# Attention with a threshold mask and an expert layer: the mask's bias on VectorE, the weights loaded as float32 and cast on the chip

## Chip, cores and metric

One Trainium2 chip, one of its cores. The time is the device time of one execution in microseconds (us), as the median of a kernel's timed executions.

## The reference, cut to what matters

```python
def _attn_ref(q, k, v, tau):                      # 8 x 8 heads, 576 rows, head size 64
    scores = scale * np.matmul(q, k.transpose(0, 1, 3, 2))
    thresh = np.max(scores, axis=-1, keepdims=True) - tau
    scores = np.where(scores >= thresh, scores, -1000000000.0)
    ...                                           # softmax
    return np.matmul(attn, v)

def _moe_ref(x, w_in, w_out):                     # x: 4608 x 512, w_in: 512 x 2048, w_out: 2048 x 512
    h = x @ w_in
    relu6 = np.clip(h + 3.0, 0.0, 6.0)
    g = h * relu6 / 6.0
    return g @ w_out
```

## The kernel before

The program is one loop of 144 slots, nine for each group of four heads. A slot takes 128 queries of two heads through the softmax, and puts matrix work of the expert layer between. The scores are compared with their row's maximum through a *bias*, `tau - scale*max`, that a Prelu on ScalarE (the mask) adds: what falls below zero is multiplied by 1e30.

```python
    def load_v(b):                                # float32 in memory, bfloat16 on the chip
        ...
            vcasts.append(lambda g=g: nc.gpsimd.dma_start(out=vm[:, g * 4:g * 4 + 4, :], in_=v[b, ...]))
        ...                                       # two of vm, two of vr for each batch
    def load_weights():                           # 32 pieces of 128 x 512
        for n4 in range(4):
            for ki in range(KI):
                casts.append(lambda n4=n4, ki=ki: nc.gpsimd.dma_start(out=w_in_sb[...], in_=moe_w_in[...]))
        ...                                       # and 16 of w_out

    def sm_max(sl):
        ...
        for i, ps in enumerate(sl.tiles):         # two heads
            nc.vector.tensor_scalar(out=sl.s[...], in0=ps[...], ..., op1=Alu.max, accum_out=sl.m[:, i:i + 1])
            nc.gpsimd.tensor_scalar(out=sl.bias[:, i:i + 1], in0=sl.m[:, i:i + 1], scalar1=-scale, scalar2=tau,
                                    op0=Alu.mult, op1=Alu.add)

    def sm_norm(sl):
        for i in range(2):
            nc.gpsimd.tensor_scalar(out=pn[:, i, :], in0=sl.s[:, i, :], scalar1=sl.rinv[:, i:i + 1], ...)
        ...
        if not sl.on_chip:                        # every second slot before 21: TensorE transposes instead
            nc.sync.dma_start_transpose(out=sl.dst, in_=pn[...])

    load_quad(0)                                  # the loads of q and k, by the sync queue
    start(loads, 5)
    load_v(0)                                     # only lists the loads of v; the loop starts them
    load_weights()
    ...
    queue[0].tiles = scores(0, 0)
    for n, sl in enumerate(queue):
        now = n
        ...
        if slot == 0 and g == 1 and b + 1 < B:
            load_v(b + 1)                         # from the third batch on, its four loads go out in slots 0 to 3
        ...                                       # exp(prev), sm_max(sl), h, ReLU, gate, o
        for i in range(2):
            sm_mask(sl, i)
        ...                                       # transpositions, attention x V, the next scores
        if prev is not None:
            sm_norm(prev)
        flush()
        start(loads, 1)
        if n < 4 or n > 12:
            start(vcasts, 1)
        if n > 3:
            start(casts, 1 if n < 24 else 2)
        prev = sl
```

## Time and profile before

| | before |
|---|---|
| time, median (lowest to highest) | 560.16 us (559.52 to 560.89) |
| span and mean granted TensorE clock of the profiled run | 558.7 us, 0.996 |
| busy: TensorE, VectorE, ScalarE, GpSimd | 530.6, 424.7, 469.7, 305.3 us |
| first mask | 9.71 us |
| slots 4-14, 14-18, 18-23 | 29.51, 13.79, 15.19 us |
| slots 23-31, 31-36 | 29.74, 17.27 us |
| slots 36-143, then the tail | 373.87, 57.3 us |

Slots are dated from ScalarE's timeline, by the first mask activation of each: "slots 14-18" runs from the mask of slot 14 to that of slot 18. Where one slot's time is given ("slot 16 took"), it runs from the mask of the slot before to its own. The start, the stages (0-4 took 12.30 us) and the tail add up to the span. So a change can be booked by stage, and each stage has its own limit.

### The profile page before, as it was taken

How to read it: one execution, taken by the hardware profiler on the slowest of the kernel's cores; microseconds unless marked ns; L12 is line 12 of the kernel's file. 1: busy time of each engine (PE TensorE's matmuls, PEld its weight loads, DVE VectorE, ACT ScalarE, POOL GpSimd, SP SyncE). 2: the span in 40 equal slices, each digit the busy share in tenths (PEclk: the TensorE clock that was granted, in tenths of full speed). 3: DMA queues.
4: the chain of work that ended last, by engine and by line, in shares of the span. 5: the costliest groups of instructions: out<-in, count | busy, mean ns of one | idle time of the engine just before them, and what ended most of it. 6: DMA issues, size and time to landing. Idle time of an engine off the chain costs nothing.

```text
span 558.7 us, 11624 instructions
## 1 busy us (share of the span) xinstructions
PE 530.6 (95%) x3829; PEld 309.2 (55%) x3870; DVE 424.7 (76%) x1041; ACT 469.7 (84%) x999; POOL 305.3 (55%) x646
## 2 busy tenths in 40 slices
PE   8899798799999999999999999999999999999997
PEld 6655455555555555655555555655555565654663
DVE  3787686787878788887978788887978798883440
ACT  4899899798889999899898999899898999984440
POOL 2788878854556555755556555755556555561000
PEclk9999899999999999999999999999999999999999
DMA  5999979976789869978689889977689865454102
GB/s 121 137 120 173 196 128 190 204 142 126 137 158 152 152 136 157 178 149 146 130 148 152 173 131 160 175 147 147 131 145 166 150 144 114 100 109 94 38 20 76
DMA packets 286348, 77.52 MB, mean 139 GB/s; under 512 B 269264, under 2 KB 281808, under 8 KB 286288
## 3 DMA queue, kind: packets, MB, share of 16 engines
q1 hardware_dynamic: 267680, 67.47, 65.3%
q0 software_dynamic: 17408, 8.92, 13.6%
q8 instruction: 30, 0.49, 0.4%
q10 hardware_dynamic: 1200, 0.39, 0.3%
q14 instruction: 30, 0.25, 0.1%
HBM read 36.70 MB, written 9.44 MB: 83 GB/s over the span
## 4 chain that ended last, share of the span: by engine, by line
PE 55%; DVE 11%; ACT 8%; issue 4%; SPq 3%; DMA 2%; POOL 2%; DVEq 0%; POOLq 0%
PE h L357 17%; PE o L386 16%; PE s L260 15%; DVE s L281 5%; PE av L327 3%; ACT s L289 3%; ACT s L294 3%; DMA nq<-in_q_dram 2%; DVE g L374 2%; DVE r L368 2%; ACT r L366 1%; PE s L266 1%; PE tp L214 1%; SPq L310 1%; POOL pn L302 1%
## 5 line engine op out<-in xcount | busy, mean ns | idle before, releaser
L302 POOL TENSOR_SCALAR pn<-s,rinv 128x576 bf16<-128x576 f32 x288 | 211.6, 745 | 133.1 <-DVE rinv L297 57.3
L289 ACT ACTIVATE s<-s,bias 128x576 f32<-128x576 f32 x288 | 206.9, 766 | 36.3 <-POOL bias L284 35.2
L281 DVE TENSOR_SCALAR_CACHE_REDUCE s<-s 128x576 f32<-128x576 f32 x288 | 205.9, 752 | 40.3 <-PE s L260 29.9
L294 ACT ACTIVATE s<-s 128x576 f32<-128x576 f32 x288 | 192.7, 671 | 0.3
L260 PE MATMUL s<-kT,qT 64*128 64x288 f32 x1024 | 169.7, 430 | 5.1 <-DVE s L281 2.8
L357 PE MATMUL h<-xT,w_in_sb 128*128 128x320 bf16 (+1 forms) x1024 | 144.9, 287 | 5.9 <-DVE g L374 5.0
L386 PE MATMUL o<-w_out_sb,g 128*128 128x512 bf16 x535 | 133.5, 379 | 5.2 <-DVE osb L394 3.0
L357 PEld LDWEIGHTS <-w_in_sb 128*128 128x128 bf16 x1024 | 92.1, 97 | 68.9 <-issue 31.9
L374 DVE SCALAR_TENSOR_TENSOR g<-r,h 128x512 bf16<-128x512 f32 (+1 forms) x128 | 96.4, 755 | 41.7 <-ACT r L366 39.9
L260 PEld LDWEIGHTS s<-kT,qT 64*128 64x128 f32 x1024 | 93.7, 186 | 60.9 <-DVE s L281 24.0
L284 POOL TENSOR_SCALAR bias<-m 128x1 f32<-128x1 f32 x288 | 54.4, 189 | 66.6 <-DVE s L281 45.8
L386 PEld LDWEIGHTS <-g 128*128 128x128 bf16 x576 | 55.6, 98 | 57.4 <-issue 9.0
L366 ACT ACTIVATE r<-h,three 128x640 f32<-128x640 f32 (+1 forms) x74 | 54.4, 736 | 20.6 <-PE h L357 19.9
L294 ACT ACTIVATION_READ_ACCUMULATOR s<-s 128x1 f32 x288 | 54.2, 188 | 0.0
L368 DVE TENSOR_SCALAR r<-h 128x512 f32<-128x512 f32 (+1 forms) x54 | 40.5, 751 | 0.0
L394 DVE TENSOR_SCALAR osb<-o 128x512 f32<-128x512 f32 x31 | 21.0, 676 | 21.4 <-PE o L386 21.4
L327 PE MATMUL av<-pT,vm 128*64 128x512 bf16 x256 | 34.6, 393 | 2.0 <-ACT kT L204 2.0
L327 PEld LDWEIGHTS <-vm 128*64 128x64 bf16 x512 | 18.0, 111 | 25.3 <-issue 18.8
L297 DVE RECIPROCAL rinv<-rsum 128x2 f32<-128x2 f32 x144 | 23.0, 160 | 11.3 <-ACT s L294 10.5
L339 DVE CAST xT<-av 128x512 bf16<-128x512 f32 x32 | 21.8, 681 | 6.6 <-PE av L330 6.3
L281 DVE DVE_READ_ACCUMULATOR s<-s 128x1 f32 x288 | 23.9, 83 | 0.0
L266 PE MATMUL s<-kT,qT 64*64 64x288 f32 x256 | 20.1, 415 | 0.7 <-DVE s L281 0.7
(44 smaller groups left out, 241.4 us busy)
## 6 DMA issues: line engine op xcount, KB each, us to landing
km<-in_k_dram SPq DMA_DIRECT2D x64, 128.0 KB, 3.0
out_dram<-osb SPq DMA_DIRECT2D x31, 256.0 KB, 2.4
nq<-in_q_dram SPq DMA_DIRECT2D x96, 72.0 KB, 2.7
vm<-in_v_dram POOLq DMA_DIRECT2D x16, 256.0 KB, 5.6
w_in_sb<-in_moe_w_in_dram POOLq DMA_DIRECT2D x16, 128.0 KB, 4.3
w_out_sb<-in_moe_w_out_dram POOLq DMA_DIRECT2D x16, 128.0 KB, 4.5
pT<-pn SPq DMA_TRANSPOSE x119, 3.4
nq<-in_q_dram SPq DMA_DIRECT2D x14, 128.0 KB, 4.4
```

Source lines behind the costliest of these rows:

```text
L260: nc.tensor.matmul(tiles[a][:, hf, 0:HALF], qT_of(pair)[a * 64:(a + 1) * 64, t * P:(t + 1) * P], keys(pair, a, hf), start=True, stop=True)
L281: nc.vector.tensor_scalar(out=sl.s[:, i, :].rearrange("p (a b) -> p a b", a=2), in0=ps[:, :, 0:HALF], scalar1=1.0, scalar2=None, op0=Alu.m ...
L284: nc.gpsimd.tensor_scalar(out=sl.bias[:, i:i + 1], in0=sl.m[:, i:i + 1], scalar1=-scale, scalar2=tau, op0=Alu.mult, op1=Alu.add)
L289: nc.scalar.activation(out=s, in_=s, func=Act.Prelu, bias=sl.bias[:, i:i + 1], scale=scale, alpha=REJECT)
L294: nc.scalar.activation(out=s, in_=s, func=Act.Exp, accum_out=sl.rsum[:, i:i + 1])
L302: nc.gpsimd.tensor_scalar(out=pn[:, i, :], in0=sl.s[:, i, :], scalar1=sl.rinv[:, i:i + 1], scalar2=1.0, op0=Alu.mult, op1=Alu.mult)
L327: nc.tensor.matmul(ps[a * 64:(a + 1) * 64, :], vm[:, 2 * hp + a, c * D:(c + 1) * D], pT[:, 5 * a + c, cols], start=(c == 0), stop=False)
L357: nc.tensor.matmul(hps[:, n, 0:w], w_in_sb[:, ki, (ni + n) * P:(ni + n + 1) * P], xT[b][:, ki, c0:c0 + w], start=(ki == 0), stop=(ki == KI ...
L366: nc.scalar.activation(out=r, in_=hps, func=Act.Relu, bias=three[:])
L368: nc.vector.tensor_scalar(out=r, in0=hps, scalar1=3.0, scalar2=0.0, op0=Alu.add, op1=Alu.max)
L374: nc.vector.scalar_tensor_tensor(out=gbuf[:, ni:ni + 2, c0:c0 + w], in0=r, scalar=6.0, in1=hps, op0=Alu.min, op1=Alu.mult)
L386: nc.tensor.matmul(o_ps[0], gbuf[:, ni, mt * P:(mt + 1) * P], w_out_sb[:, ni, :], start=(ni == 0), stop=(ni == NI - 1))
```

## The change

Its intent: GpSimd's queue makes masks wait in the stages in which weights load. So the bias goes to the engine that makes the maximum, and the weights no longer need GpSimd to build a casting DMA. They come as float32 through the sync queue into six staging buffers, and GpSimd casts each piece two slots later.

```diff
+    w_pool = ctx.enter_context(tc.tile_pool(name="wp", bufs=6))
...
-                casts.append(lambda n4=n4, ki=ki: nc.gpsimd.dma_start(
-                    out=w_in_sb[:, ki, n4 * 512:(n4 + 1) * 512],
-                    in_=moe_w_in[ki * P:(ki + 1) * P, n4 * 512:(n4 + 1) * 512]))
+                casts.append(lambda n4=n4, ki=ki: stage(
+                    w_in_sb[:, ki, n4 * 512:(n4 + 1) * 512],
+                    moe_w_in[ki * P:(ki + 1) * P, n4 * 512:(n4 + 1) * 512]))
... (w_out in the same way)
+    def stage(dst, src):
+        w = w_pool.tile([P, 512], F32, tag="w", name="w")
+        nc.sync.dma_start(out=w[:], in_=src)
+        staged.append((now, dst, w))
+
+    def cast_staged():
+        while staged and staged[0][0] <= now - 2:
+            _, dst, w = staged.pop(0)
+            nc.gpsimd.tensor_copy(out=dst, in_=w[:])
...
-            nc.gpsimd.tensor_scalar(out=sl.bias[:, i:i + 1], in0=sl.m[:, i:i + 1], scalar1=-scale, scalar2=tau,
+            nc.vector.tensor_scalar(out=sl.bias[:, i:i + 1], in0=sl.m[:, i:i + 1], scalar1=-scale, scalar2=tau,
...
             sm_norm(prev)
+        cast_staged()
         flush()
```

More of the change, by code (lines that the diff above doesn't have):

```diff
@@ L76 @@
     vcasts = []
+    staged = []
     def load_quad(quad):
@@ L142, in load_weights @@
             for ki in range(KI):
-                casts.append(lambda n4=n4, ki=ki: nc.gpsimd.dma_start(
-                    out=w_in_sb[:, ki, n4 * 512:(n4 + 1) * 512],
-                    in_=moe_w_in[ki * P:(ki + 1) * P, n4 * 512:(n4 + 1) * 512]))
+                casts.append(lambda n4=n4, ki=ki: stage(
+                    w_in_sb[:, ki, n4 * 512:(n4 + 1) * 512],
+                    moe_w_in[ki * P:(ki + 1) * P, n4 * 512:(n4 + 1) * 512]))
         for ni in range(NI):
-            casts.append(lambda ni=ni: nc.gpsimd.dma_start(
-                out=w_out_sb[:, ni, :], in_=moe_w_out[ni * P:(ni + 1) * P, :]))
+            casts.append(lambda ni=ni: stage(w_out_sb[:, ni, :], moe_w_out[ni * P:(ni + 1) * P, :]))
+    def stage(dst, src):
[6 more added lines that the diff above has]
+            nc.gpsimd.tensor_copy(out=dst, in_=w[:])
     def start(jobs, n):
@@ L152, in start @@
             jobs.pop(0)()
+    now = -1
     load_quad(0)
@@ L187, in kT_of @@
         return qkT[pair // 2][1][:, pair % 2, :]
-    now = -1
     turn = 0
```

## The prediction

> **What bounds the kernel now.** I read the page first (busy shares, the 40 slices, the groups), then the busy time by stretch, then the chain of waits and the timelines where a stretch looked unlike its neighbours. A slot is one step of the program: 128 queries of two heads, 144 slots in all; I date slots by the first mask activation (L289) of each in ScalarE's timeline.
>
> ```profile
> PE 530.6 (95%) x3829; PEld 309.2 (55%) x3870; DVE 424.7 (76%) x1041; ACT 469.7 (84%) x999; POOL 305.3 (55%) x646
> ...
> PE   8899798799999999999999999999999999999997
> ...
> POOL 2788878854556555755556555755556555561000
> ```
>
> The shares mix stages. POOL (GpSimd) is 55% busy overall, but 70 to 80% in slices 2 to 8 (14 to 112 us), which is where TensorE shows its only 7s before the end. Those are the slots in which the weights are loaded. The table by stretch (us; PE, PEld, DVE, ACT, POOL busy) shows the two regimes:
>
> ```profile
> 50.00:60.00 10.00, 7.23 (x52) 3.75 (x51) 8.22 (x25) 8.32 (x19) 9.22 (x19) 0.97 1.26 167
> ...
> 100.00:110.00 10.00, 7.59 (x68) 4.59 (x70) 6.40 (x17) 8.41 (x19) 8.68 (x17) 1.00 1.39 208
> ...
> 300.00:350.00 50.00, 49.11 (x376) 28.46 (x379) 42.00 (x107) 46.71 (x102) 27.97 (x61) 1.00 0.89 148
> ```
>
> At 50 to 60 us TensorE is 72% busy and POOL 92%; from 125 us on TensorE is 98% busy and POOL 56%. In the steady stage the chain of waits is TensorE after TensorE:
>
> ```profile
> 255.46 1.19 PE h L357 x8
> 256.66 1.73 PE o L386 x8
> 258.38 1.17 PE s L260 x8
> 259.55 1.19 PE h L357 x8
> ```
>
> In the loading stage it goes through POOL. Its queue is in order, so the bias (L284) of a slot stands behind the normalisation (pn) of an earlier slot and the descriptors of the DMAs issued there, and ScalarE's mask waits for it:
>
> ```profile
> 96.98 0.74 POOL vm L122
> ...
> 97.72 0.81 POOL w_out_sb L147 x2
> ...
> 98.86 0.19 POOL bias L284
> 99.06 0.02 issue
> 99.08 1.44 ACT s L289 x2
> ```
>
> VectorE had finished the maximum of that slot at 96.59 (timeline), so the bias came 2.3 us late, and ScalarE's timeline has it idle 1.40 us before 99.08. The list of waits gives ScalarE's idle time for the bias, one line for each of the stretches 8 to 42, 42 to 78, 78 to 125 and 125 to 500 us (total, times, longest):
>
> ```profile
> ACT s L289 <- POOL bias L284: 4.9, 7, 2.4
> ACT s L289 <- POOL bias L284: 4.0, 7, 1.1
> ACT s L289 <- POOL bias L284: 5.1, 7, 1.4
> ACT s L289 <- POOL bias L284: 20.7, 47, 1.5
> ```
>
> So 14.0 us fall in the early stages, where they cost time, and 20.7 in the one that TensorE bounds, where they mostly do not.
>
> **What the Trainium skill says.** (1) "DMA: Bandwidth & Descriptors", SWDGE vs HWDGE vs iDMA: a DMA that casts must be issued by GpSimd, where software builds the descriptors; plain ones from the sync queue are built in hardware. The trace agrees: each weight DMA (L143, L147) holds POOL for 536 to 596 ns. (2) "VectorE: DVE Perf Modes", The DRAIN you can't avoid: a same-engine read after write needs a semaphore. The changed program has it: every bias waits for VectorE's own semaphore. The trace agrees that dependence costs time (below). (3) "SBUF — State Buffer", Who interferes with whom: VectorE and GpSimd share a port pair, and a tensor_scalar in a two-port mode blocks, or is blocked by, a whole GpSimd instruction. Whether a one-element operation takes that mode, no run here shows. (4) The DMA page again, Issuing engines are not separate DMA queues: the same 16 engines serve all queues, so the weights' traffic is not lightened; the trace has the DMA share at 1.26 and 1.39 in the two early stretches above.
>
> **The change part by part.**
>
> *Removed from POOL:* 288 bias operations of 189 ns, 54 us, and 32 descriptor builds of about 0.57 us, 18 us. *Added to POOL:* 32 casts of 128x512. The normalisation of 128x576 takes 745 ns; in proportion I put a cast at 0.65 us (an estimate), 21 us together. POOL falls from 305 to about 254 us. More important, ScalarE no longer waits for that queue.
>
> *Added to VectorE:* 288 bias operations, between the two maxima of a slot and after the second. Here dependence costs more than the operation:
>
> ```profile
> 260.36 0.08 DVE L281 DVE_READ_ACCUMULATOR s<-s 128x1 f32 x1
> 260.36 0.75 DVE L281 TENSOR_SCALAR_CACHE_REDUCE s<-s 128x576 f32<-128x576 f32 x1
> 261.04 0.08 DVE L281 DVE_READ_ACCUMULATOR s<-s 128x1 f32 x1
> 261.04 0.82 DVE L368 TENSOR_SCALAR r<-h 128x640 f32<-128x640 f32 x1
> 261.89 0.82 DVE L374 SCALAR_TENSOR_TENSOR g<-r,h 128x640 bf16<-128x640 f32 x1
> ```
>
> An operation that depends on nothing before it starts 0.68 us after a maximum of 0.75 started: they overlap. The gate (L374), which reads what L368 wrote, starts 0.03 after its end. A bias must wait for the accumulator read, 0.76 after the maximum's start, plus 0.03; it lasts about 0.16 (the smallest arithmetic in the trace, the reciprocal of 128x2 on L297, has a median of 158 ns), and the next operation can overlap its last 0.08. So the next starts at 0.87 instead of 0.68: 0.19 us for each bias, 0.37 to 0.38 for a slot, 54 us of VectorE's time in all. As busy time less, since part is waiting: I expect VectorE at about 460 us.
>
> *Moved to the sync queue:* 32 loads of 256 KB, at about 0.62 us of issuing each (its other loads take 1.25 for two), 20 us in the slots 4 to 29. They stand in order behind the DMA transposes (1.3 us), which wait for pn.
>
> *Stage 1, slots 4 to 23 (22.0 to 80.5 us).* ScalarE's floor is a mask pair and an exp pair, 1.35 + 1.34 = 2.70 us. Slots 14 to 18 (48.15 to 65.31) take 3.43 each, because POOL does bias, pn, vm or vr and w, 3.3 us, without a gap; without that loop I give them 2.85: 5 x 0.58 = 2.9 us. The other 14 take 2.90 to 3.04; VectorE, 2.4 us of busy time a slot there (46.4 us in the 19.5 slots from 20 to 80 us), rises to 2.75, so it is as tight as ScalarE, and I credit 0.1 each: 1.5 us.
> *Stage 2, slots 23 to 31 (80.5 to 110.2).* 3.72 us each. ScalarE's work is 2.70, 0.62 for a ReLU in half of them, and some copies: 3.2. I credit 0.35 of the 0.5: 2.8 us.
> *From these, the casts take back something:* a load issued at the end of slot n follows pn(n-1), a transpose (1.3), other loads (1.3 to 2.6) and itself (0.6), and lands some 4 us later (3.0 to 4.4 are the medians of such loads): 7 to 8.5 us after pn(n-1). Its cast follows pn(n+1), two slots or 5.7 us later. So POOL can stand for 1 to 2 us at a cast, and pn behind it is late; in the slots up to 22 TensorE transposes every second pn itself and has little spare. I take off 1.5 us. Early stages together: 2.9 + 1.5 + 2.8 - 1.5 = 5.7 us gained.
>
> *Stage 3, slots 36 to 143 (127 to 505 us).* 3.49 us a slot, TensorE bound. VectorE is busy 42.0 of 50, 2.93 a slot; with 0.37 it has 0.19 left. What it can hurt is the gate: the next slot's h matmuls wait for it, since h has one buffer. I took from the two timelines, for each gate, the time from its end to the start of the next h. Where ScalarE does the ReLU, the gate had been waiting for it (25.6 us in 48 waits, 0.53 each), which absorbs 0.37. Where VectorE does (48 gates), 22 have under 0.4 us to spare and the shortfalls against 0.37 sum to 5.0 us. Against that, earlier masks pull some late ReLUs forward: I give 1.5 back. Loss 3.5 us. The tail after 505 us holds no bias and no load and stays.
>
> **Sum:** 560.2 - 5.7 + 3.5 = 558 us.
>
> **The rivals.** *A: POOL's queue was all that mattered,* and VectorE's additions hide. For it: VectorE is 76% busy and waits 25 us for scores in the steady stage. Against: the 22 gates with no spare time. It would give 560 - 7 to 8, about 552. *B: VectorE becomes the second bound of the steady stage:* backlog of one slot meets the next in slots with an output copy (0.6) and a transposition. For it: 0.19 us left of 3.49. Against: a backlog needs consecutive heavy slots, and slot 8 of each nine has no gate. At 0.06 us more a slot it costs another 6 us: 564 to 566. *C: the weights arrive late* and casts hold POOL for long: the sync queue is nearly full in slots 22 to 29 (transpose, loads and two weights, about 4.3 us a slot). For it: DMA share 1.39. Against: pn's four buffers, and the first w_out is only needed at slot 31. The early gain would vanish: 563. *D: the one-element operation takes the shared port* and stands behind pn's 0.75 us: up to 10 or 20 us more, above 571. Nothing in the trace speaks for it.
>
> **Range and chances.** The two terms have opposite signs and similar size, so I stay near the old time: 558 us, 550 to 566 for A to C. Faster by over 2% (below 549.0) needs more than all the early waiting, 8%; slower by over 2% (above 571.4) needs B and C together, or D: 6%; within 2%, 86%.
>
> **What would show it.** Right: no wait of ScalarE for POOL; bias on VectorE near 160 ns, each taking 0.19 us from the row of operations; VectorE near 460 us, POOL near 254; slots 14 to 18 under 3 us and 23 to 31 near 3.4; more and longer waits of h for the gate after 125 us, slots there 3.52 to 3.53. Wrong: a bias far from 160 ns, or stretched beside pn (D); steady slots unchanged (A) or above 3.55 (B); POOL idle for long before casts and early slots no shorter (C).

## More of the kernel before

GpSimd's timeline, TensorE's and ScalarE's of the kernel before (start, duration, engine, line, operation, and in brackets how long the engine had been idle and what ended that):

```profile
5.06 0.63 PE L214 MATMUL tp<-identf,km 128*128 128x128 f32 x4 [0.45 <-DMA km<-in_k_dram]
...
9.48 0.19 POOL L284 TENSOR_SCALAR bias<-m 128x1 f32<-128x1 f32 x1 [8.17 <-DVE s L281]
...
9.71 0.78 ACT L289 ACTIVATE s<-s,bias 128x576 f32<-128x576 f32 x1 [2.44 <-POOL bias L284]
```

TensorE transposes the first keys at 5.06, and GpSimd has nothing to do before the first bias at 9.48. Behind that bias, in the same queue, stands the first load of v; GpSimd began it at 10.40.

## The result, and the profile after

The changed kernel takes 572.19 us (four runs, 571.43 to 573.15) against 560.16. The ratio is 1.0215, 95% interval 1.0201 to 1.0230: slower by just over 2%, and above the predicted range. All results are correct.

Line numbers of the new kernel are 11 higher from the scores on (mask L300, bias L295, pn L313, gate L385, h L368). Its page:

```profile
PE 539.9 (95%) x3870; PEld 313.6 (55%) x3870; DVE 462.8 (81%) x1329; ACT 475.6 (83%) x999; POOL 251.8 (44%) x358
...
PE   7899789989999999999999999999999999999997
PEclk8999699999999999999999999999999999999999
...
POOL 1556665585335434544345444544445445442000
```

The busy times came out as predicted: VectorE 462.8 (predicted 460), GpSimd 251.8 (254), and GpSimd's digits 2 to 8 fell from 7 and 8 to 5 and 6. The sign that something else went wrong is in the clock row, where the slices are 14.3 us wide: an 8 in the first and a 6 in the fifth (57 to 71 us). The booking by stage gives:

| | before | after | difference | predicted |
|---|---|---|---|---|
| first mask | 9.71 | 13.56 | +3.85 | 0 |
| slots 0-4 | 12.30 | 12.48 | +0.18 | 0 |
| 4-14 | 29.51 | 29.43 | -0.08 | parts of -1.5 and -2.9 |
| 14-18 | 13.79 | 17.86 | +4.07 | most of -2.9, part of +1.5 |
| 18-23 | 15.19 | 15.88 | +0.69 | parts of -1.5 and +1.5 |
| 23-31 | 29.74 | 25.61 | -4.13 | -2.8 |
| 31-36 | 17.27 | 20.88 | +3.61 | 0 |
| 36-143 | 373.87 | 377.60 | +3.73 | +3.5 |
| tail | 57.3 | 57.3 | -0.02 | 0 |
| sum | | | +11.9 | -2.2 |

The five slots to which the prediction gives -2.9 run from the mask of slot 13 (48.15) to that of slot 18 (65.31), one slot more than "14-18". Over these five the difference is +3.67.

Each stage is read from one profiled run, so it matters how far a stage moves by chance. Two kernels of the experiments, e7 and e10, issue the same instructions as the kernel before up to slot 36. Against it, their first mask came 0.50 and 0.98 us later, 14-18 took 0.73 and 1.23 less, 31-36 took 0.00 and 1.05 more, and the other early stages moved by under 0.1. One source of this is TensorE's clock. The kernel before has a spell at half clock in stage 14-18, from 59.35 to 62.76 by its clock records; its windows (columns as further below, the clock is the third number from the end):

```profile
58.00:60.00 2.00, 0.98 (x10) 0.32 (x4) 1.96 (x7) 1.85 (x3) 1.82 (x5) 0.84 1.35 209
60.00:62.00 2.00, 1.99 (x13) 1.05 (x15) 0.85 (x4) 1.52 (x5) 1.74 (x5) 0.50 1.37 228
62.00:64.00 2.00, 2.00 (x14) 0.81 (x10) 0.69 (x1) 2.00 (x6) 1.73 (x3) 0.81 1.40 216
```

Slot 18 took 3.91 us there; it took 2.68 in e5, e7 and e10, which have the same bias and no such spell at that point. So 1.2 us of the time that the prediction put down to GpSimd's loop in these slots were a spell of half clock.

The table shows one gain and four losses that are clear of this; three of the losses were not in the working or were far larger than in it. The four losses, one after the other:

**The start.** The same three engines in the new kernel:

```profile
1.45 0.93 POOL L124 DMA_DIRECT2D vm<-in_v_dram  x1
...
7.48 0.63 PE L225 MATMUL tp<-identf,km 128*128 128x128 f32 x4 [2.86 <-DMA km<-in_k_dram]
...
13.56 0.78 ACT L300 ACTIVATE s<-s,bias 128x576 f32<-128x576 f32 x1 [3.32 <-DVE bias L295]
```

The first load of v is no longer held behind a bias, and leaves at 1.45 instead of 10.40. The first keys then reach TensorE 2.42 us later. The other 1.43 us come after that: TensorE's next transpositions (of q) took 1.06 us instead of 0.60, and the recorded clock is 0.59 and 0.56 in the windows 8 to 10 and 10 to 12 us, where it was 1.00 before.

**Slots 14-18.** TensorE, GpSimd and ScalarE at slot 16:

```profile
57.98 0.61 POOL L159 CAST w_in_sb<-w 128x512 bf16<-128x512 f32 x1 [2.58 <-DVE bias L295]
59.38 1.47 POOL L313 TENSOR_SCALAR pn<-s,rinv 128x576 bf16<-128x576 f32 x2
...
60.19 1.43 PE L329 MATMUL pt<-identb,pn 128*128 128x128 bf16 x9 [2.85 <-POOL pn L313]
62.40 2.29 PE L271 MATMUL s<-kT,qT 64*128 64x288 f32 x8
...
65.87 1.58 ACT L300 ACTIVATE s<-s,bias 128x576 f32<-128x576 f32 x2 [4.83 <-DVE bias L295]
```

GpSimd stood idle for 2.58 us at a cast, with the next pn behind it in the queue. (The profile puts that wait down to a bias of VectorE's, which the cast does not read. The cast needs the transfer of w: the one issued at 53.27 landed at 57.93, by the trace, and the cast began at 57.98.) TensorE stood idle 2.85 us for that pn. The windows (us; PE, PEld, DVE, ACT, POOL busy, then clock, DMA share, GB/s) show what followed:

```profile
60.00:65.00 5.00, 4.70 (x23) 2.99 (x23) 1.63 (x3) 1.04 (x4) 3.63 (x6) 0.50 1.24 242
65.00:70.00 5.00, 4.67 (x31) 2.22 (x31) 3.45 (x14) 3.00 (x7) 3.85 (x6) 0.52 1.29 202
```

For 10 us TensorE ran at half its clock, though it was 94% busy. Eight score matmuls took 2.29 us; at full clock and with no wait among them they take 1.24. Slot 16 took 7.59 us.

The Trainium skill, "TensorE: Matmul & The Clock Gate", Part 1: The HAM clock gate, says that TensorE's clock is halved after an idle window of about 3.4 us, and comes back after about as long of steady work. In the length of a spell the traces agree: leaving out the last 10 us of each run, every spell at half clock in the fourteen clock records lasted 3.41 or 3.42 us, or two or three times that (59.56 to 69.80 here, 10.24 us). In what starts a spell they do not. TensorE had been idle for 2.2 us (from 57.33) when the clock fell here, and in the 3.4 us ahead of the spell in the kernel before it was idle for 0.90 us at the longest (58.39 to 59.29). Nor does the idle time decide it alone: after 2.62 us in e3 (114.41 to 117.03) and 2.03 in the kernel before (102.92 to 104.96) the clock stayed at 1.00. That the wait at slot 16 brought this spell is likely, since e3's profile repeats it (2.71 us of idle time, then 10.24 at half clock), but it is not shown.

**Slots 31-36** give back most of what 23-31 gained; the wait there is shown with experiment e1.

**Slots 36-143.** TensorE's waits for the gate in this stage, before and after (engine, line, releaser: total us, times, longest):

```profile
PEld L357 <- DVE g L374: 5.2, 8, 0.8
...
PE h L357 <- DVE g L374: 2.4, 7, 0.4
```

```profile
PEld L368 <- DVE g L385: 12.1, 19, 1.0
...
PE h L368 <- DVE g L385: 3.4, 8, 0.5
PEld s L271 <- DVE bias L295: 10.4, 25, 0.4
```

TensorE's weight loads waited 12.1 us for the gate instead of 5.2, its matmuls 3.4 instead of 2.4. The two overlap, so their sum is not time lost. The last line is new: the weight loads of the scores now wait for the bias too. To see which slots the waits for the gate belong to, I added up both kinds by slot (windows around each h, 7.8 and 15.3 us in all): before, they lie ahead of the h of slots 3 (3.9 us), 7 (2.9) and 4 and 6 (1.0). After, they lie ahead of slots 3 (7.4), 7 (5.9) and 5 (2.0). These follow the gates of slots 2, 6 and 4, whose ReLU VectorE does itself. How much of the +3.73 comes by the gate and how much by the scores is not shown.

### The profile page after: what moved, and what is told of

It is laid out like the page before. It is cut to its first block, busy times and chain, and to the rows that moved or that the text cites. A ratio compares the mean times of both kernels' runs of the same rounds, so it can differ in the third digit from the quotient of the medians.

```text
span 570.6 us, 11793 instructions
## 1 busy us (share of the span) xinstructions
PE 539.9 (95%) x3870; PEld 313.6 (55%) x3870; DVE 462.8 (81%) x1329; ACT 475.6 (83%) x999; POOL 251.8 (44%) x358
## 4 chain that ended last, share of the span: by engine, by line
PE 57%; DVE 21%; ACT 8%; issue 5%; POOL 4%; DMA 4%; SPq 2%; DVEq 0%; POOLq 0%; ACTq 0%
PE s L271 16%; PE o L397 14%; PE h L368 14%; DVE s L292 10%; PE av L338 4%; ACT s L300 3%; DVE g L385 3%; ACT s L305 3%; POOL pn L313 2%; DVE r L379 2%; PE s L277 2%; DMA nq<-in_q_dram 2%; DVE bias L295 2%; PE tp L225 1%; PE warm L177 1%
## 5 line engine op out<-in xcount | busy, mean ns | idle before, releaser
L313 POOL TENSOR_SCALAR pn<-s,rinv 128x576 bf16<-128x576 f32 x288 | 210.9, 744 | 248.6 <-DVE rinv L308 114.6
L292 DVE TENSOR_SCALAR_CACHE_REDUCE s<-s 128x576 f32<-128x576 f32 x288 | 215.4, 748 | 38.1 <-PE s L271 32.3
L300 ACT ACTIVATE s<-s,bias 128x576 f32<-128x576 f32 x288 | 214.4, 769 | 26.8 <-DVE bias L295 21.8
L271 PE MATMUL s<-kT,qT 64*128 64x288 f32 x1024 | 173.8, 433 | 4.9 <-DVE s L292 2.4
L368 PE MATMUL h<-xT,w_in_sb 128*128 128x320 bf16 (+1 forms) x1024 | 145.1, 287 | 6.7 <-DVE g L385 4.9
L397 PE MATMUL o<-w_out_sb,g 128*128 128x512 bf16 x576 | 141.2, 379 | 4.7 <-DVE osb L405 4.4
L271 PEld LDWEIGHTS s<-kT,qT 64*128 64x128 f32 x1024 | 96.6, 187 | 61.3 <-DVE s L292 19.1
L368 PEld LDWEIGHTS <-w_in_sb 128*128 128x128 bf16 x1024 | 91.3, 98 | 70.2 <-issue 29.6
L385 DVE SCALAR_TENSOR_TENSOR g<-r,h 128x512 bf16<-128x512 f32 (+1 forms) x128 | 96.2, 752 | 14.4 <-ACT r L377 10.1
L295 DVE TENSOR_SCALAR bias<-m 128x1 f32<-128x1 f32 x288 | 44.3, 154 | 10.0
L225 PE MATMUL tp<-identf,km 128*128 128x128 f32 x128 | 19.8, 278 | 2.9 <-DMA km<-in_k_dram 2.9
```

The lines of the kernel that those rows point to most:

```text
L271: nc.tensor.matmul(tiles[a][:, hf, 0:HALF], qT_of(pair)[a * 64:(a + 1) * 64, t * P:(t + 1) * P], keys(pair, a, hf), start=True, stop=True)
L292: nc.vector.tensor_scalar(out=sl.s[:, i, :].rearrange("p (a b) -> p a b", a=2), in0=ps[:, :, 0:HALF], scalar1=1.0, scalar2=None, op0=Alu.m ...
L295: nc.vector.tensor_scalar(out=sl.bias[:, i:i + 1], in0=sl.m[:, i:i + 1], scalar1=-scale, scalar2=tau, op0=Alu.mult, op1=Alu.add)
L300: nc.scalar.activation(out=s, in_=s, func=Act.Prelu, bias=sl.bias[:, i:i + 1], scale=scale, alpha=REJECT)
L368: nc.tensor.matmul(hps[:, n, 0:w], w_in_sb[:, ki, (ni + n) * P:(ni + n + 1) * P], xT[b][:, ki, c0:c0 + w], start=(ki == 0), stop=(ki == KI ...
L385: nc.vector.scalar_tensor_tensor(out=gbuf[:, ni:ni + 2, c0:c0 + w], in0=r, scalar=6.0, in1=hps, op0=Alu.min, op1=Alu.mult)
```

## The experiments

Three theories stood at the beginning. *Casts:* late transfers hold GpSimd at the casts (rival C of the prediction), all the rest is small. *Start:* the freed load of v delays the first keys. *VectorE:* the bias costs there far more than its 0.19 us (rivals B and D). Twelve kernels ran, four at a time, each group on one chip with its own runs of the kernel before. Two more, which cast four slots later from twelve buffers, could not be built: they need 24 KB in each partition, and 12.8 KB were left.

### e1 and e2: one half of the change each

e1, from the kernel before:
```diff
-            nc.gpsimd.tensor_scalar(out=sl.bias[:, i:i + 1], ...
+            nc.vector.tensor_scalar(out=sl.bias[:, i:i + 1], ...
```

> The bias moved to VectorE alone; the weights stay cast DMAs issued by GpSimd. Theory 1, from the two traces: the 12 us of the change are four separate things: +3.9 at the start (GpSimd no longer waits for the first bias, so the first load of v is issued at 1.5 instead of 10.4 us and delays the first q and k; first mask at 13.6 instead of 9.7), +4 and +4 from casts that wait for their load and hold pn back (slots 15 to 18 and 31 to 36), +3.7 in the slots 36 to 143 from the bias on VectorE, and -4 in slots 23 to 31. Then this kernel has the start's and the steady stage's loss and the gains, without the casts: 561 to 565 us. Theory 2, VectorE is the bound everywhere and the bias alone is the whole loss: 570 to 573. Theory 3, the weights are the whole loss (their bytes as float32, their place in the sync queue): 556 to 560.

Measured: 570.96 us (567.21 to 574.49), ratio 1.0190 [1.0139, 1.0241]. Start +4.64, slots 14-18 **-1.43**, 18-23 +2.22, 23-31 -4.05, 31-36 +5.10, 36-143 +3.77.

e2, from the changed kernel:
```diff
-            nc.vector.tensor_scalar(out=sl.bias[:, i:i + 1], ...
+            nc.gpsimd.tensor_scalar(out=sl.bias[:, i:i + 1], ...
```

> The weights by the sync queue and cast by GpSimd, the bias left on GpSimd. Theory 1: start as before (first mask at 9.7), slots 36 to 143 as before (3.49 us each), but waits of casts now also hold the bias: 564 to 570 us. Theory 2 (the bias on VectorE is the whole loss): 558 to 562. Theory 3 (the weights are): 570 to 573.

Measured: 571.92 us (569.99 to 572.53), ratio 1.0202 [1.0179, 1.0226]. Start +0.09, 4-14 +3.14, 14-18 +1.13, 23-31 **+7.23**, 31-36 +0.74, 36-143 -0.38.

What follows: each half alone costs about as much as both together, in different places. Both times missed the range of my first theory (561 to 565, 564 to 570) and lie inside that of the theory that makes this half the whole loss. The stages speak against it, as neither half has the losses of the other. The start, the steady stage and the give-back at 31-36 belong to the bias. The stall at 14-18 needs the casts. With the casts but without the bias moved, the biases stand behind waiting casts and the stages of the weights get worse; the moved bias is what turns +7.23 into -4.13 in 23-31. (In e2's stage 23-31 ScalarE waited 11.4 us for the bias, up to 5.2 at a time.) In e1 the bias alone gives -4.05 there, with the weights' DMAs still built by GpSimd. The losses do not add up, so halves of a change cannot be booked by subtracting.

e1 also shows the give-back most clearly. The remainder of slot 26's pn, pR, is transposed by a DMA, and TensorE reads it in slot 31. The issue of that transposition in the kernel before, then e1's timelines:

```profile
99.05 3.22 SPq L310 DMA_TRANSPOSE pR<-pn  x1
```

```profile
105.86 3.37 SPq L310 DMA_TRANSPOSE pR<-pn  x1
...
114.34 0.32 PE L327 MATMUL ar<-pR,vm 128*64 128x64 bf16 x8 [1.93 <-DMA pR<-pn]
116.39 2.32 PE L357 MATMUL h<-xT,w_in_sb 128*128 128x320 bf16 x8
119.44 1.43 ACT L289 ACTIVATE s<-s,bias 128x576 f32<-128x576 f32 x2
```

Before, TensorE read pR at 109.42, 10.4 us after its issue, and did not wait. In e1 pR went out 6.8 us later: TensorE read it 8.5 us after the issue, and had waited 1.93 us for it at the last wait. Then the clock fell again, to 0.50 in the window 116 to 118 us: h took 2.32 us, against 1.26 at full clock, and slot 32 took 7.71. The changed kernel has the same waits, shorter (1.8 us of its weight loads and 1.3 us of its matmuls, for pR), and slot 32 takes 5.58.

### e3 and e5: the load of v at the start

e3, from the changed kernel, holds the loads of v back by one slot; e5, from the kernel before, sends the first one before the first slot, and so the next three one slot earlier:
```diff
# e3
-        if n < 4 or n > 12:
+        if 0 < n < 5 or n > 12:
# e5
+    start(vcasts, 1)
+
     queue = []
```

> The changed kernel with the first four loads of v started one slot later, so that the first stands behind the first pn in GpSimd's queue, as the bias held it in the kernel before. Theory 1: first mask back at 9.7 to 10 us, total 3.5 to 4 us less: 568 to 569. If the late start was the profiled run's chance, or had another cause: 571 to 573.

> The kernel before with one thing changed: the first load of v is issued before the first slot, ahead of the first bias in GpSimd's queue, as it comes to stand in the changed kernel. If the late start of the changed kernel is this load's traffic beside the first q and k (in the changed kernel TensorE's first transposition of k starts at 7.5 instead of 5.1 us): first mask 2.4 to 4.6 us later, 562 to 565 us. If the start is late for another reason (in the run with v held, k came on time, but TensorE's float32 matmuls took double time, and the first mask was still 2.6 us late): 559.5 to 561.5.

Measured, e3: 570.43 us (567.69 to 572.27), ratio 1.0165 [1.0127, 1.0204], start +2.60. e5: 564.92 us (560.54 to 565.67), ratio 1.0068 [1.0025, 1.0110], start +4.87. The rest of the stages cancel but for 0.3 us: 14-18 -1.22, and 18-23 +1.59 with a spell at half clock in it (71.20 to 74.62). One of its four runs took 560.54, no longer than the kernel before, so the loss is not in every run. Its start:

```profile
1.46 0.93 POOL L122 DMA_DIRECT2D vm<-in_v_dram  x1
...
7.10 1.09 PE L214 MATMUL tp<-identf,km 128*128 128x128 f32 x4 [2.48 <-DMA km<-in_k_dram]
```

e5 reproduces the loss at the start with the bias and the weights as they were, so it is the load of v. All five kernels that send it early (the changed one, e1, e4, e5, e6) begin the first transposition at 6.87 to 7.48, the nine others at 5.05 to 5.34. The late keys are 2.04 us of e5's loss; the other 2.83 come with transpositions at half rate, and for that part the load is not shown to be the cause.

e3 gave back less than that theory asks, in its profiled run, which is the slowest of the four (567.69, 568.99, 571.88, 572.27; the theory asked for 568 to 569). Its keys came on time (first transposition at 5.34), but that transposition took 1.09 us instead of 0.63, and those after it 1.06. Such half-rate starts were also seen where keys came at 5.06 to 5.11 (e7, e8, e10), with a start of +0.50 to +0.98, and not in e9 and e11 (0.63; +0.10 and -0.01). Why TensorE starts at half rate in some executions stays open: the clock records show 1.00 there. The Trainium skill, in the same part of "TensorE: Matmul & The Clock Gate", warns that these records were seen to be unreliable and that the window of the gate runs freely; these durations beside a recorded 1.00 agree with the first.

### e4 and e6: late casts

From the changed kernel, e4 casts three slots after the load; e6 issues the weight load ahead of the transposition of its slot:
```diff
# e4
-        while staged and staged[0][0] <= now - 2:
+        while staged and staged[0][0] <= now - 3:
# e6
+        if n > 3:
+            start(casts, 1 if n < 24 else 2)
         if prev is not None:
             sm_norm(prev)
...
-        if n > 3:
-            start(casts, 1 if n < 24 else 2)
```

> The changed kernel with every cast three slots after its load instead of two, the same six buffers. Theory 1: the waits of casts (14.2 us of GpSimd idle before them) mostly vanish, slot 16 (7.6 us) and slot 32 (5.6 us) become ordinary: 564 to 567 us. If the DMA engines or the sync queue's own order are what is late, beyond one slot, or the stalls have another cause: 570 to 573.

> The changed kernel with each weight load issued before the slot's DMA transpose instead of after it, cast two slots later as before. If the casts were late because a load stood in the sync queue behind a transpose that waits for pn: GpSimd's idle time before casts (16.8 us) falls under 6, slots 14 to 18 lose their 4 us, 566 to 569 us. If the DMA engines were late with the data: idle time and stall as before, 571 to 573.

Measured, e4: 570.38 us (568.1 to 573.0), ratio 1.0182 [1.0140, 1.0222]; slots 14-18 at -1.35, but 31-36 at +5.17 (slot 32: 7.91). e6: 570.24 us (569.63 to 574.85), ratio 1.0193 [1.0140, 1.0246]; 14-18 at -1.43, 18-23 +2.24, 23-31 only -0.46, 31-36 +2.77. GpSimd's idle time ahead of the casts was 9.8 (w_out), 4.4 (w_in) and 2.6 us (put down to another cause) in the changed kernel; in e4 4.3, 4.7 and about 1.5. In e6 it was still 11.2 us, a clear miss: I had expected under 6. e4's time was a miss too (564 to 567 expected).

What follows: the stall at 14-18 (+4.07) is the casts, since a slot more of room, or an earlier load, turns it into the gain that e1 has without casts. It is worth about 5.5 us. Much of that was lost further on: e4 gives 1.6 us more back at slots 31-36 and takes 0.9 us more at 18-23, and e6 moved its waits into 23-31. By their four runs neither kernel is clearly faster than the changed one.

### e7 and e10: the steady stage by itself

From the kernel before, VectorE makes the bias from slot 36 on: two operations a slot in e7; one on 128x2 after both maxima in e10.
```diff
# e7
-            nc.gpsimd.tensor_scalar(out=sl.bias[:, i:i + 1], ...
+            (nc.vector if now >= 36 else nc.gpsimd).tensor_scalar(out=sl.bias[:, i:i + 1], ...
# e10
+        if now >= 36:
+            nc.vector.tensor_scalar(out=sl.bias[:], in0=sl.m[:], scalar1=-scale, scalar2=tau,
```

> The kernel before with the bias on VectorE in slots 36 to 143 alone. Theory 1 (the loss there is VectorE's dependent operations delaying the gate, 3.75 us in four runs): 563.5 to 564.5 us, and the earlier slots as before. If the loss there came of the state in which the early stage leaves the queues: 560 to 561.

> The kernel before with the bias on VectorE in slots 36 to 143, but one operation of 128x2 a slot, after both maxima, in place of two of 128x1. If the loss there (3.7 us with two) goes with the number of dependent operations: about half, 1.5 to 2.2 us, 561.5 to 562.8 us. If a bias of two elements takes the port that GpSimd shares and stands behind pn, it lasts longer than 0.16 us in the groups, and the loss is 4 us or more. If the loss came of the first bias between the two maxima alone: near 0.

Measured, e7: 564.44 us (564.05 to 565.13), ratio 1.0080 [1.0056, 1.0103]; slots 36-143 +3.69. e10: 561.82 us (560.67 to 562.43), ratio 1.0019 [0.9995, 1.0042]; slots 36-143 +1.19. So the steady loss is the bias on VectorE and nothing else (+3.69 alone, +3.73 in the change). One operation instead of two leaves a third of it, less than the half (1.5 to 2.2) that I had expected in this stage. e10 takes away an operation and also the bias between the two maxima, so it does not tell which of these counts. The operations themselves, as the lists of one line's instructions have them (minimum, median, maximum in ns), in the changed kernel and in e10:

```profile
L295 DVE TENSOR_SCALAR bias<-m x288: 152/154/156, 13.4 to 513.9; 128x1 f32<-128x1 f32 x144
```

```profile
L288 DVE TENSOR_SCALAR bias<-m x108: 168/169/401, 127.9 to 503.1; 128x2 f32<-128x2 f32 x108
```

The one-element bias never left 152 to 156 ns, whatever GpSimd did: rival D of the prediction is refuted. The two-element one was stretched to as much as 401. Of the 108, 22 took over 200 ns, and each of the 22 began while GpSimd was in an instruction (11 times a pn, 11 times the building of a load of v). Beside a pn it ended about 0.02 us after the pn. None of the other 86 lay beside a GpSimd instruction for more than 0.13 us. For two elements that agrees with what the prediction quotes from "SBUF — State Buffer"; of the one-element biases of the changed kernel 103 began with GpSimd busy for at least 0.13 us more, and none was stretched.

### e8, e9, e11 and e12: is there a version that wins?

e8, from the kernel before, has the bias on VectorE only in slots 1 to 35. e9 adds to e8 that the loads of v go out from slot 5 of their group (slots 32 to 35 for the third batch, instead of 27 to 30). e11 is the kernel before with that move of v alone. e12 is the changed kernel with both, and with casts three slots after the load.
```diff
# e8, e9, e12
+            (nc.vector if 0 < now < 36 else nc.gpsimd).tensor_scalar(out=sl.bias[:, i:i + 1], ...
# e9, e11, e12
-        if slot == 0 and g == 1 and b + 1 < B:
+        if slot == 5 and g == 1 and b + 1 < B:
# e12
+        while staged and staged[0][0] <= now - 3:
```

> The kernel before with the bias on VectorE in slots 1 to 35 alone, so the first load of v stays behind the first bias. By the sums of the run with the bias alone on VectorE: start as before, slots 23 to 31 4 us shorter, slot 32 longer by about 5 (TensorE waits for the transposed remainder pR, which lands as late as before), slots 36 on as before: 559 to 563 us. If the 4 us are kept: 555 to 557.

> As the run before it, and the loads of v from the second quarter on start five slots later (32 to 35 instead of 27 to 30; first used at slot 44), away from the weights. If the stall at slot 32 is the DMA engines' load (pR lands 8.5 us after its issue there, 4.8 in the median): the stall falls from 7.7 to under 5 us, 554 to 558 us. If it is the order of the sync queue: no change against the run before it.

> The control of the fastest run so far (556.9): the kernel before with only the loads of v five slots later, the bias on GpSimd throughout. If that run's gain needs both parts: 559 to 561 us here. If the later loads of v are the gain: 556 to 557.5.

> The changed kernel repaired as far as the runs tell: bias on VectorE in slots 1 to 35 alone, loads of v five slots later, casts three slots after their loads. Against the same with the weights as cast DMAs (556.9 us): if the weights by the sync queue are neutral once they don't hold GpSimd, 556 to 558; if they still cost (4.3 us of waiting in slots 23 to 31 of the run with the later casts), 558 to 562; if they help, under 556.

Measured:

| | median (lowest to highest) | ratio, 95% | start | 14-18 | 18-23 | 23-31 | 31-36 | 36-143 |
|---|---|---|---|---|---|---|---|---|
| e8 | 559.61 (558.98 to 563.15) | 1.0002 [0.9966, 1.0039] | +0.61 | -1.43 | +1.05 | -4.05 | +2.85 | -0.05 |
| e9 | 556.87 (556.17 to 557.55) | 0.9940 [0.9919, 0.9962] | +0.10 | -1.43 | +2.66 | -4.06 | +1.46 | -1.51 |
| e11 | 558.26 (556.79 to 559.46) | 0.9956 [0.9926, 0.9986] | -0.01 | +0.34 | 0.00 | -2.03 | +0.31 | -1.20 |
| e12 | 557.53 (555.93 to 560.55) | 0.9951 [0.9912, 0.9989] | +0.24 | -1.36 | +1.04 | -4.14 | +2.28 | -1.12 |

e8, e9 and e12 came within their expected ranges; e11 fell between its two.

What follows: with the first bias left on GpSimd the start is whole again (+0.10 to +0.61), as the load of v is held once more. Without the bias from slot 36 on, the steady loss is gone. What is left in e8 is the early stages alone: -5.5 in 14-18 and 23-31, of which +3.9 are given back in 18-23 and 31-36. (Of the 5.5, 1.2 are the spell that the profile of the kernel before has in 14-18.) In e9 the give-back at 31-36 halves when the loads of v no longer run in slots 27 to 30 (slot 32 takes 4.20 in e9 and e12, 5.59 in e8), so those loads are part of what delays pR. Whether it is their traffic, or GpSimd's time to build them ahead of pn, is not told apart. The loss at 18-23 goes with TensorE's clock in e1 and e9: 0.50 in the window 72 to 74 us of e1, where slot 20 took 4.52, and 0.51 in 68 to 70 us of e9, where it took 4.96. e5, with bias and weights as before, has such a spell there too (slot 20: 4.13), so this part is not shown to be the bias. Without a spell, in e8 and e12, the loss at 18-23 is about 1.0.

e9 is the fastest of all, 0.6% below the kernel before, its interval clear of 1. But e11, which only moves the loads of v, gets 0.4%, and the intervals overlap: that moving the bias in the early slots adds anything is not shown. e11's own gain lies in 23-31 and 36-143. e12's four runs spread over 4.6 us; within that, the weights' new path, once repaired, shows neither gain nor loss.

## Why the prediction was wrong, by its own steps

Its sum was -2.2 us, and +11.9 were measured. Three terms failed: the casts' 1.5 us were about 5.5, and the start (+3.85) and the give-back at 31-36 (+3.61) stood in it at 0. A smaller fourth is the gain in slots 4 to 23. The prediction gave 6% to a time above 571.4, and only by B and C together or by D; B (steady slots above 3.55 us) and D did not come true. Step by step:

- **The busy times and the cost of one bias: right.** A bias takes 154 ns (predicted near 160), the maxima of a slot start 0.86 us apart (0.87), VectorE 462.8 us (460), GpSimd 251.8 (254), a cast 610 ns (650).
- **Steady stage, +3.5: right in place and size.** +3.73, in e7 +3.69; 3.53 us a slot as predicted, with more waits ahead of the gates that VectorE's ReLU precedes. Its two terms (5.0 lost, 1.5 given back) cannot be measured apart, and the scores' waits for the bias were not in the working. The size of the sum may owe something to luck.
- **Slots 23-31, -2.8: right, more than predicted (-4.13).** The bias alone does it: e1 and e8 have -4.05 with the descriptors still built by GpSimd.
- **Slots 14-18, -2.9: mostly not there.** Over the prediction's five slots the kernels with the bias moved and no stall (e1, e4, e6, e8, e9, e12) take 15.33 to 15.41 us. The kernel before takes 17.17 with its spell at half clock, e5 and e10, with its bias and no spell, 15.95 and 15.94. So by these profiles 0.6 us are the bias's, and 1.2 of the 1.8 were a spell that the prediction took for GpSimd's loop.
- **The 14 other early slots, -1.5: absent.** (14 slots at 0.1 us make 1.4.) They took 0.32 us more up to the mask of slot 13, and 0.69 more in 18-23. The waits of ScalarE that I credited there did not set the time.
- **"I take off 1.5 us" for the casts: mis-sized.** The prediction had the geometry right, a cast 1 to 2 us before its data and a pn behind it; GpSimd waited 2.58. It left out what can follow on TensorE: 2.85 us of waiting, and 10 us at half clock. The term was about 5.5 us in this place alone. Rival C had named it, and its size (the whole early gain of 5.7 vanishes) was nearer.
- **The start: absent from the sum.** The working read the bias only as something that waits behind DMAs. At the first slot it was the DMA that waited behind the bias, and that order kept a load of v out of the way of the first keys. +3.85; of it 2.42 are the late keys, shown by e5 (2.04 with this edit alone) and by e2 and e8, in which the first bias stays on GpSimd and the keys are on time. The cause of the other 1.43 stays open.
- **The give-back at 31-36: absent.** I booked a faster stage 2 as gain, and did not ask which transfer it would run into. +3.61 of the 4.13 came back: 2.2 in slot 32, where TensorE waits for pR, and the rest in slots 34 to 36, where the cause was not looked for.

Still open are what starts a spell at half clock, the half-rate starts without a recorded fall of the clock, and why e1, e3 to e6, e8 and e12 spread over 4.2 to 7.3 us from run to run, where the kernel before spreads over 1.4 to 2.4. Spells are part of the last: in e1, e4, e5, e6 and e12 the fastest run has the highest mean clock and the slowest the lowest (e1: 567.21 us at 0.997, 574.49 at 0.991); in e3 it is not so. One spell of 3.41 us at half clock can cost up to 1.7 us (an estimate from these two numbers), so stages that differ by less need more than one profile.

## What to carry to other kernels

An instruction in an in-order queue also holds back what stands behind it: before moving one, ask which DMA it was delaying, and what that DMA will meet when it is free, above all in the first microseconds. Book a predicted gain only after naming the next transfer that the faster stage will wait for. And where TensorE may be left idle for 2 to 3 us, allow for time at half clock after the gap: here it was 3.4 or 10.2 us long after some such gaps, and absent after others.

## What the Trainium skill lacked or had wrong

- "TensorE: Matmul & The Clock Gate", Part 1: an idle window of about 3.4 us halves the clock and about 3.4 us of work restores it. Here the length agrees for single spells (3.41 us). But the clock fell after 2.2 us of idle time at slot 16, and in the kernel before with none longer than 0.90; it stayed up after 2.62 in e3; and at slot 16 it stayed at half for 10.24 us, 9.6 of them after work had resumed, with TensorE 94% busy.
- The same page says that clock records can be unreliable, with a clock that is stuck low. Here is the opposite case: transpositions of 128x128 at half rate (1.08 or 1.09 us for four instead of 0.63) with a recorded clock of 1.00, in e1, e3, e4, e5, e7, e8 and e10.
- "SBUF — State Buffer", Who interferes with whom: it tells which operations can take the shared ports, and no case as small as these. A tensor_scalar of 128x1 stayed at 152 to 156 ns in all 288 cases, 103 of them with GpSimd busy; one of 128x2 ranged from 168 to 401.
- No page that I read warns that moving an instruction off an in-order queue releases the DMAs behind it: here a load went out at 1.45 instead of 10.40 us, and the first keys came 2.42 us later.
